# Split low halves, a norm shared with ScalarE, and a new list of steps in a Fourier transform with two MLPs on one core

## The chip, the core and the metric

The kernel runs on one core of a Trainium2 chip. The core has a matrix engine (TensorE, PE in the profile; PEld is its weight load), VectorE (DVE), ScalarE (ACT), GpSimd (POOL) and SyncE (SP), which here only issues DMAs. Each engine works through its own list of instructions in order and waits on semaphores for the others. The metric is the device time of one launch in microseconds (us), as the median of several runs.

## The reference, cut to what matters

```python
X = np.fft.fft(np.fft.fft(x, axis=1), axis=2).real            # x: 2 x 3008 x 256, float32
h = X @ w_in;  g = h * np.clip(h + 3.0, 0.0, 6.0) / 6.0;  y = g @ w_out      # w_in 256 x 2048
xn = y / np.sqrt(np.mean(y * y, -1, keepdims=True) + 1e-06) * rms_g
g2 = xn @ w_gate;  out = (g2 / (1 + np.exp(-g2)) * (xn @ w_val)) @ w_out2    # w_gate 256 x 1536
```

The weights come in as 8-byte floating point numbers and are turned into float32 on the chip ("decode").

## The kernel before, in words

Every matrix product keeps about float32 precision by splitting each operand into a high part (`S.copy` to a rounded type, on ScalarE) and a low part (`sub`, operand minus high part, on GpSimd or, for steps with a mark, on VectorE), and by three matrix multiplications: high by high, low by high, high by low (`PASSES`).

The transform along the sequence folds the 3008 points of each batch into sums and differences (`fold` for the first batch, `late_fold` and `late_split` for the second), multiplies them by tables of cosines and sines (`smm`, L435) and copies the result out of PSUM (`evac`, `evac_x`). A column that does not fit the tables (`fold_x128`, `split_x128`, `xmm`, `evac_x`) goes its own way, through `xb`. The transform along the model dimension is multiplied into `w_in` (`wmm`).

The first MLP is 96 **items** (`item1`; numbers 0 to 95 in the list of steps): six blocks of 502 columns, each with its mirrored columns, by 16 slices of 128 hidden units. An item has 6 matrix multiplications into two PSUM banks E and O (L532), a vector operation that adds the odd column (L536), a sum and a difference (L538, L539), two Relu on ScalarE (L544), two minimum-and-multiply on VectorE (L547), the high part on ScalarE (L550), the low part on GpSimd (L268, called from L553) and 12 matrix multiplications into four accumulating banks (L564).

The second MLP is 144 items (`item2`; +0 to +143 in the list): 12 blocks of 502 columns by 12 slices. Ahead of a block stands its **norm** (`rms`, rms0 to rms11): Square on ScalarE, the mean over 256 by a matrix multiplication with ones, an integer estimate of the reciprocal root, three Newton rounds of three vector operations each (L654, L656, L658), two scalings (L661), high and low part. The blocks of rms0 and rms1 serve items +0 to +23, and so these two norms lie among the last items of the first MLP.

The order of the work is not left to a scheduler: each function is a generator, and the string `STEPS` names, token by token, which one goes on to its next `yield`. An engine's instructions stand in the order in which the tokens issue them. A token with a quote mark puts the subtraction of that step on VectorE instead of GpSimd. PSUM is full: E0, O0, E1, O1 are used by items in turn, acc0 to acc3 by the sums. `sl(tag)` names a place in SBUF; a place that is taken again makes its next writer wait for the last reader. Lines L78 to L164 hold the list.

Of the kernel before, what the change touches and what calls it, by code (L numbers as in the profile page):

```python
# [13 lines left out]
ALU = mybir.AluOpType  # L14
P = 128
# [75 lines left out]
    lf2 17 16 19 18 19 18 17 lf2 19 18 19 18 20 lf2 18 19 21 20 ls00 20 21 lm01 18 20 21 19 20 22 20 ls00 21 19 22 21 20
    22 23 21 22 21 20 23 pq02 23 pq02' 23 21 22 23 22 22 24 23 25 24 24 23 22 25 24 25 24 25 23 24 25 24 26 23 27 26 25 26
# [8 lines left out]
    56 55 cw01 57 56 lw11 cw01 57 56 cw01 58 57 56 59 58 cw10 cw10 57 56 59 58 59 58 57 cw10 59 58 59 58 60 cw10 58 59
    lw20 61 60 cw10 60 cw10 61 58 60 61 59 cw11 cw10 60 cw11 62 60 61 cw11 60 59 62 61 62 63 61 cw11 62 lw21 61 60 63 pq12
    63 cw11 62 pq12 63 61 62 63 cw11 64 62 cw20 cw11 63 cw20 65 63 62 64 65 64 65 64 63 cw20 65 64 65 66 64 63 cw20 64 67
    66 66 65 67 cw20 65 64 66 67 rms0 66 cw20 67 rms0 68 66 cw20 67 65 cw21 66 68 cw21 69 67 68 67 66 69 68 cw21 69 67
    cw21 69 68 rms1 69 70 68 rms1 69 68 71 70 cw21 70 71 69 68 70 71 70 cw21 71 72 70 cw21 71 69 70 72 72 73 72 rms0 rms0
    71 70 72 71 73 73 74 72 73 72 71 74 74 73 74 72 73 74 73 75 74 74 76 75 75 73 76 75 76 75 76 74 75 76 75 77 76 78 77
    76 77 75 78 77 78 77 78 76 77 78 77 79 78 80 79 78 79 77 80 79 80 79 80 78 79 80 79 81 80 82 81 80 81 79 82 81 82 81
    82 79 rms0 82 rms0 83 81 rms0 rms0 84 81 83 rms0 80 tw1 83 81 82 84 rms0 83 82 84 83 rms0 82 84 rms0 83 rms0 84 83 85
    rms0 84 86 84 85 83 86 85 rms0 85 86 84 tw2 rms0 86 85 rms0 85 87 rms0 85 86 lw30 rms0 87 88 86 rms0 86 85 88 87 cw30
    88 87 86 cw30 88 rms1 87 rms1 89 87 cw30 88 87 89 90 88 cw30 88 87 89 lw40 cw30 90 89 90 cw30 88 89 90 89 90 89 91 90  # L110
# [57 lines left out]
def fft_mlp_mlp_kernel(ctx: ExitStack, tc: tile.TileContext, x, xq, mats, dmat, w_in, w_out, w_gate, w_val, w_out2, rms_g, out):  # L168
# [671 lines left out]
```

## Time and profile before

| | us |
|---|---|
| median of 3 runs | 1140.87 (1140.39 to 1141.67) |
| profiled execution, its own time | 1142.43 |
| its span, first to last instruction | 1140.7 |
| PE busy | 1067.5 (94%) |
| PE weight loads busy | 870.2 (76%) |
| DVE busy | 832.6 (73%) |
| ACT busy | 504.8 (44%) |
| POOL busy | 483.0 (42%) |
| mean granted TensorE clock | 0.982 |

A busy share is a mean over stages with different limits, so the rows further down cut the span into stretches. In a row of waits, "A <- B" says that engine A sat idle until the instruction of engine B ended; in a row of the timeline the bracket gives the idle time just before it. Busy times of one engine can overlap by some hundredths of a microsecond, since an instruction starts while the one before it drains.

### The profile page before, as it was taken

How to read it: one execution, taken by the hardware profiler on the slowest of the kernel's cores; microseconds unless marked ns; L12 is line 12 of the kernel's file. 1: busy time of each engine (PE TensorE's matmuls, PEld its weight loads, DVE VectorE, ACT ScalarE, POOL GpSimd, SP SyncE). 2: the span in 40 equal slices, each digit the busy share in tenths (PEclk: the TensorE clock that was granted, in tenths of full speed). 3: DMA queues.
4: the chain of work that ended last, by engine and by line, in shares of the span. 5: the costliest groups of instructions: out<-in, count | busy, mean ns of one | idle time of the engine just before them, and what ended most of it. 6: DMA issues, size and time to landing. Idle time of an engine off the chain costs nothing.

```text
span 1140.7 us, 12657 instructions
## 1 busy us (share of the span) xinstructions
PE 1067.5 (94%) x4572; PEld 870.2 (76%) x4572; DVE 832.6 (73%) x1223; ACT 504.8 (44%) x754; POOL 483.0 (42%) x292
## 2 busy tenths in 40 slices
PE   3778788999998899899999999999999999999998
PEld 3656566888886678678778888888888888888887
DVE  6899998787779997998789874383746657374532
ACT  6556435655565565455444433232323233332332
POOL 0056444656755566465234333333323333332332
PEclk9889998999999999999999999999999999999999
DMA  8640132002431100110220000000000000000000
GB/s 268 208 145 1 37 77 41 1 1 41 100 77 39 55 38 1 38 55 1 79 89 36 37 1 19 1 19 1 19 19 1 19 1 19 16 3 19 1 19 19
DMA packets 18895, 47.21 MB, mean 41 GB/s; under 512 B 3914, under 2 KB 6986, under 8 KB 17946
## 3 DMA queue, kind: packets, MB, share of 16 engines
q1 hardware_dynamic: 15808, 36.92, 9.9%
q0 software_dynamic: 3024, 9.48, 3.7%
q8 instruction: 36, 0.59, 0.2%
q14 instruction: 27, 0.22, 0.1%
HBM read 33.53 MB, written 8.27 MB: 37 GB/s over the span
## 4 chain that ended last, share of the span: by engine, by line
PE 70%; DVE 21%; issue 3%; DMA 3%; ACT 1%; POOL 1%; SPq 0%; DVEq 0%; ACTq 0%; POOLq 0%
PE acc L709 16%; PE E L687 16%; PE O L687 16%; PE acc L564 13%; DVE R L547 4%; PE E L532 3%; PE O L532 3%; DVE T L536 2%; DVE O L539 2%; DVE E L538 2%; DMA J<-in_x 1%; PE E L435 1%; PE O L435 1%; POOL LO L268 1%; DVE c_p L258 1%
## 5 line engine op out<-in xcount | busy, mean ns | idle before, releaser
L268 POOL TENSOR_TENSOR LO<-R,HI 128x1004 fp32r<-128x1004 f32 x96 | 233.8, 2448 | 193.2 <-ACT HI L550 185.4
L564 PE MATMUL acc<-HI,B 128*128 128x502 f32 x768 | 250.9, 394 | 0.1
L693 DVE TENSOR_TENSOR R<-T,E 128x502 f32<-128x502 f32 x144 | 97.2, 675 | 177.9 <-ACT T L690 173.6
L268 POOL TENSOR_TENSOR HI<-R,HI 128x502 fp32r<-128x502 f32 x87 | 119.0, 1367 | 239.0 <-ACT HI L699 238.9
L564 PEld LDWEIGHTS acc<-HI,B 128*128 128x128 f32 x768 | 147.0, 191 | 30.6 <-ACT HI L550 0.5
L564 PE MATMUL acc<-LO,B 128*128 128x502 f32 x384 | 153.5, 400 | 10.5 <-POOL LO L268 10.3
L687 PE MATMUL E<-J,B 128*128 128x502 f32 x576 | 147.3, 391 | 0.0
L687 PE MATMUL O<-J,A 128*128 128x502 f32 x576 | 146.6, 389 | 0.0
L550 ACT CAST HI<-R 128x1004 fp32r<-128x1004 f32 x96 | 99.2, 1034 | 97.6 <-DVE R L547 63.2
L268 POOL TENSOR_TENSOR LO<-R,LO 128x502 fp32r<-128x502 f32 x57 | 77.4, 1358 | 148.2 <-ACT LO L699 148.2
L690 ACT ACTIVATE T<-E 128x502 f32<-128x502 f32 x144 | 84.8, 589 | 108.4 <-PE E L687 108.2
L687 PEld LDWEIGHTS E<-J,B 128*128 128x128 f32 x576 | 108.9, 189 | 22.9
L687 PEld LDWEIGHTS O<-J,A 128*128 128x128 f32 x576 | 108.8, 189 | 22.5
L699 ACT CAST HI<-R 128x502 fp32r<-128x502 f32 x87 | 53.3, 613 | 141.3 <-DVE R L695 126.8
L544 ACT ACTIVATE R<-E,c_three 128x502 f32<-128x502 f32 x96 | 65.4, 682 | 97.7 <-DVE E L538 78.9
L532 PE MATMUL E<-J,A 128*128 128x502 f32 x288 | 86.4, 410 | 23.3 <-DVE R L547 22.6
L695 DVE TENSOR_TENSOR R<-R,O 128x502 f32<-128x502 f32 x144 | 97.1, 674 | 9.2
L564 PEld LDWEIGHTS acc<-LO,B 128*128 128x128 f32 x384 | 73.5, 191 | 34.4 <-POOL LO L268 19.7
L709 PE MATMUL acc<-HI,B 128*128 128x502 f32 x354 | 90.5, 391 | 0.0
L532 PEld LDWEIGHTS E<-J,A 128*128 128x128 f32 x288 | 55.0, 197 | 41.3 <-DVE R L547 29.7
L532 PE MATMUL O<-J,A 128*128 128x502 f32 x288 | 85.2, 406 | 0.0
L709 PEld LDWEIGHTS acc<-HI,B 128*128 128x128 f32 x354 | 66.8, 189 | 14.4 <-POOL HI L268 0.4
(233 smaller groups left out, 1643.1 us busy)
## 6 DMA issues: line engine op xcount, KB each, us to landing
out_dram<-H SPq DMA_DIRECT2D x24, 251.0 KB
A<-in_w_in SPq DMA_DIRECT2D x4, 1024.0 KB
W<-in_w_gate SPq DMA_DIRECT2D x6, 512.0 KB
W<-in_w_val SPq DMA_DIRECT2D x6, 512.0 KB
W<-in_w_out SPq DMA_DIRECT2D x6, 512.0 KB
PQ<-in_x SPq DMA_DIRECT2D x3, 1008.0 KB
B<-in_w_out SPq DMA_DIRECT2D x2, 1024.0 KB
YB<-in_w_out SPq DMA_DIRECT2D x2, 1024.0 KB
```

Source lines behind the costliest of these rows:

```text
L268: low[0].tensor_tensor(o, a, b, op=ALU.subtract)
L532: T.matmul(bk[:, :BL], a[:, lw, eo, fs], j[:, eo, lx], start=(n == 0), stop=(n == 2))
L544: S.activation(x, bk[:, :BL], AF.Relu, bias=c3)
L547: V.scalar_tensor_tensor(x, x, 6.0, bk[:, :BL], op0=ALU.min, op1=ALU.mult)
L550: S.copy(hi, r)
L564: T.matmul(acc[k][:, :BL], w[:, lw, f % 4, d * P:(d + 1) * P], (hi, lo)[lx][:, hf * BL:(hf + 1) * BL], start=(first and n == 0), stop=(las ...
L687: T.matmul(bk[:, :BL], w[:, lw, d, fs], j[:, d, lx], start=(m == 0), stop=(m == 5))
L690: S.activation(s, E[:, :BL], AF.Sigmoid)
L693: V.tensor_tensor(u, s, E[:, :BL], op=ALU.mult)
L695: V.tensor_tensor(u, u, O[:, :BL], op=ALU.mult)
L699: S.copy(hl[0], u)
L709: T.matmul(acc[d][:, :BL], w[:, lw, f % 4, d * P:(d + 1) * P], hl[lx], start=(f == 0 and m == 0), stop=(f == NF2 - 1 and m == 2))
```

## The change

Three edits in the functions, and a new list. In `item1` the low part is issued as two subtractions of 502 columns, each a step of its own, where it was one of 1004. In `rms` five operations of VectorE go to ScalarE: the high part of the sum of squares, the scaling with the added constant, and in each Newton round the product `-0.5*r*r`, which becomes `Square(sqrt(0.5)*r)` with the sign turned in the last operation of the round; three rounds turn the sign three times, and a negated copy of the gain (`gsn`) puts it right. A second constant (`ceps`) is set for the scaling. The list `STEPS` is planned anew from its first to its last line.

```diff
 STEPS = """
-    one dm x01 raw11 raw00 g xq x00 x00 raw01 lwi0 raw02 x02 raw10 fold1 fold1 mat11 fold1 fold1 mat00 fx sx0 fold1 sx0
...
+    one dm xq x01 raw00 x00 x00 raw01 g lwi0 raw02 fx x02 sx0 raw11 sx0 raw10 sx0 sx1 fold1 fold1 mat00 fold1 mat00 mat00
...
-    c3 = sl("c_three", [P, 1])
+    cc = sl("c_three", [P, 2])
+    c3, ceps = cc[:, 0:1], cc[:, 1:2]
     gsc = sl("c_g", [P, 2])
+    gsn = sl("c_gn", [P, 2])
...
         lo = sl(rr("LO", 2), [P, 2 * BL], F32R)
-        sub(lo, r, f32(hi))
-        yield
+        for x in range(2):
+            cs = slice(x * BL, (x + 1) * BL)
+            sub(lo[:, cs], r[:, cs], f32(hi[:, cs]))
+            yield
...
         hl = sl("LO2", [P, 2, BL], F32R)
-        V.tensor_copy(hl[:, 0], sm)
+        S.copy(hl[:, 0], sm)
...
-        V.tensor_scalar(v, p[:, :BL], 1.0 / D, EPS, op0=ALU.mult, op1=ALU.add)
+        S.activation(v, p[:, :BL], AF.Identity, scale=1.0 / D, bias=ceps)
...
             yield
-            V.scalar_tensor_tensor(a, r, -0.5, r, op0=ALU.mult, op1=ALU.mult)
+            S.activation(a, r, AF.Square, scale=math.sqrt(0.5))
             yield
             V.tensor_tensor(a, a, v, op=ALU.mult)
             yield
-            V.scalar_tensor_tensor(r, a, 1.5, r, op0=ALU.add, op1=ALU.mult)
+            V.scalar_tensor_tensor(r, a, 1.5, r, op0=ALU.subtract, op1=ALU.mult)
         for d in range(2):
             yield
-            V.scalar_tensor_tensor(xn[:, d], y1[blk][:, d, cs], gsc[:, d:d + 1], r, op0=ALU.mult, op1=ALU.mult)
+            V.scalar_tensor_tensor(xn[:, d], y1[blk][:, d, cs], gsn[:, d:d + 1], r, op0=ALU.mult, op1=ALU.mult)
...
         SY.dma_start(gsc, rms_g)
+        yield
+        V.tensor_scalar(gsn, gsc, -1.0, None, op0=ALU.mult)
```

Where the list moves instructions, three places matter. The first is the start of SP's list of DMAs. `in_x` is the input, `in_mats` the tables (YB and A tiles those of the even outputs, PQ1 those of the odd ones), `in_w_in` the first MLP's weights. Before:

```order
L212 DMA J1_10_83<-in_x 126x2048
L228 DMA PQ1_11_85<-in_mats 126x2268
L228 DMA YB1_12_87<-in_mats 126x2268
L732 DMA c_g_3_70<-in_rms_g 128x2
L726 DMA c_xq_6_73<-in_xq 126x48
L212 DMA J0_13_91<-in_x 126x1024 x2
L228 DMA YB2_14_94<-in_mats 126x2268
L247 DMA A1_15_96<-in_w_in 128x2x1024
```

Now:

```order
L733 DMA c_xq_7_74<-in_xq 126x48
L216 DMA J1_11_86<-in_x 126x2048
L232 DMA YB1_12_88<-in_mats 126x2268
L216 DMA J0_13_90<-in_x 126x1024 x2
L232 DMA YB2_14_93<-in_mats 126x2268
L739 DMA c_g_3_70<-in_rms_g 128x2
L251 DMA A1_15_96<-in_w_in 128x2x1024
L232 DMA A2_16_98<-in_mats 126x2268
```

The odd table (558.1 KB) no longer stands second, and the small `in_xq` stands first. The second place is TensorE's list around item 0 (the first rows `<-J0,A0`); acc0 and acc1 there are the odd column's product of the odd outputs (`xmm`), E and O with 376 columns the other products of the odd outputs. Before:

```order
L435 MATMUL O0_65_329<-YB2_68_353,YB0_55_270 128x376 x3
L435 MATMUL E1_69_356<-c_p9_74_378,YB0_55_270 128x376 x3
L435 MATMUL O1_70_357<-YB2_68_353,YB0_55_270 128x376 x3
L435 MATMUL acc0_57_276<-YB2_68_353,J1_28_136 128x376 x3
L435 MATMUL acc1_58_277<-YB2_68_353,J1_28_136 128x376 x3
L532 MATMUL E0_80_414<-J0_71_364,A0_59_284 128x502 x3
L532 MATMUL O0_81_415<-J0_71_364,A0_59_284 128x502 x3
```

Now:

```order
L439 MATMUL O0_64_319<-YB2_69_347,YB0_56_268 128x376 x3
L439 MATMUL E1_66_329<-c_p9_70_358,YB0_56_268 128x376 x3
L439 MATMUL O1_67_330<-YB2_69_347,YB0_56_268 128x376 x3
L536 MATMUL E0_76_388<-J0_65_327,A0_57_278 128x502 x3
L536 MATMUL O0_77_389<-J0_65_327,A0_57_278 128x502 x3
L536 MATMUL E1_78_399<-J0_65_327,A0_57_278 128x502 x3
L536 MATMUL O1_79_400<-J0_65_327,A0_57_278 128x502 x3
L439 MATMUL acc0_81_411<-A2_52_244,J1_23_116 128x376 x3
L439 MATMUL acc1_82_412<-A2_52_244,J1_23_116 128x376 x3
```

All 18 multiplications of that product now stand behind items 0 and 1; before, 12 of them stood earlier still and the last 6 in front of item 0. The third place is VectorE's list in the last items of the first MLP; W0 and LO2 are tiles of rms0, the rows with T, E, O and R belong to items. Before, from the first operation of item 84 to the last ahead of that of item 85:

```order
L536 SCALAR_TENSOR_TENSOR T0_704_3632<-X1_8_75,c_wx_4_71,E0_694_3585 128x502
L658 SCALAR_TENSOR_TENSOR W0_592_3039<-LO2_693_3583,W0_592_3039 128x502
L538 TENSOR_TENSOR E0_694_3585<-T0_704_3632,O0_695_3586 128x502
L539 TENSOR_TENSOR O0_695_3586<-T0_704_3632,O0_695_3586 128x502
L547 SCALAR_TENSOR_TENSOR R1_705_3635<-R1_705_3635,E1_690_3571 128x502
L547 SCALAR_TENSOR_TENSOR R1_705_3635<-R1_705_3635,O1_691_3572 128x502
L654 SCALAR_TENSOR_TENSOR LO2_693_3583<-W0_592_3039 128x502
L656 TENSOR_TENSOR LO2_693_3583<-LO2_693_3583,W0_592_3039 128x502
L658 SCALAR_TENSOR_TENSOR W0_592_3039<-LO2_693_3583,W0_592_3039 128x502
L547 SCALAR_TENSOR_TENSOR R0_707_3657<-R0_707_3657,E0_694_3585 128x502
L547 SCALAR_TENSOR_TENSOR R0_707_3657<-R0_707_3657,O0_695_3586 128x502
L654 SCALAR_TENSOR_TENSOR LO2_693_3583<-W0_592_3039 128x502
```

Now, in the same place:

```order
L540 SCALAR_TENSOR_TENSOR T0_716_3762<-X1_9_76,c_wx_5_72,E0_710_3741 128x502
L542 TENSOR_TENSOR E0_710_3741<-T0_716_3762,O0_711_3742 128x502
L543 TENSOR_TENSOR O0_711_3742<-T0_716_3762,O0_711_3742 128x502
L540 SCALAR_TENSOR_TENSOR T1_717_3779<-X1_9_76,c_wx_5_72,E1_714_3754 128x502
L542 TENSOR_TENSOR E1_714_3754<-T1_717_3779,O1_715_3755 128x502
L543 TENSOR_TENSOR O1_715_3755<-T1_717_3779,O1_715_3755 128x502
L551 SCALAR_TENSOR_TENSOR R0_718_3781<-R0_718_3781,E0_710_3741 128x502
L551 SCALAR_TENSOR_TENSOR R0_718_3781<-R0_718_3781,O0_711_3742 128x502
```

And now, twelve items earlier, from the first operation of item 72 to that of item 73:

```order
L540 SCALAR_TENSOR_TENSOR T0_630_3318<-X1_9_76,c_wx_5_72,E0_626_3291 128x502
L542 TENSOR_TENSOR E0_626_3291<-T0_630_3318,O0_627_3292 128x502
L543 TENSOR_TENSOR O0_627_3292<-T0_630_3318,O0_627_3292 128x502
L662 TENSOR_TENSOR LO2_629_3316<-LO2_629_3316,W0_578_3050 128x502
L664 SCALAR_TENSOR_TENSOR W0_578_3050<-LO2_629_3316,W0_578_3050 128x502
L540 SCALAR_TENSOR_TENSOR T1_634_3348<-X1_9_76,c_wx_5_72,E1_631_3323 128x502
```

A Newton round has two rows on VectorE where it had three, and the rounds of rms0 stand at items 72 to 74 where they stood at items 82 to 86.

## Rows read from the trace of the kernel before

**Rows 1.** windows; stretch, length, busy (count) of PE, PEld, DVE, ACT, POOL, clock, DMA, GB/s:

```profile
0.00:57.00 57.00, 30.96 (x128) 27.27 (x129) 41.74 (x77) 33.42 (x47) 4.56 (x8) 0.91 0.71 238
57.00:126.00 69.00, 58.67 (x231) 45.01 (x230) 67.01 (x87) 39.93 (x54) 41.38 (x16) 0.93 0.19 62
126.00:187.00 61.00, 44.76 (x165) 33.17 (x164) 57.45 (x80) 24.08 (x34) 27.80 (x18) 0.92 0.32 70
187.00:216.00 29.00, 29.00 (x122) 23.75 (x122) 21.61 (x34) 18.82 (x27) 16.13 (x8) 0.94 0.01 2
216.00:322.00 106.00, 106.00 (x478) 88.80 (x476) 80.62 (x129) 59.84 (x84) 66.67 (x42) 1.00 0.25 49
322.00:421.00 99.00, 89.49 (x379) 71.09 (x379) 90.05 (x132) 58.66 (x84) 61.22 (x29) 0.98 0.13 43
421.00:462.00 41.00, 41.00 (x181) 33.82 (x180) 31.24 (x51) 21.82 (x30) 24.56 (x11) 1.00 0.04 13
462.00:538.00 76.00, 70.54 (x295) 55.61 (x294) 70.66 (x103) 39.97 (x54) 39.97 (x19) 0.98 0.10 35
538.00:577.00 39.00, 38.33 (x164) 30.29 (x162) 31.81 (x50) 18.23 (x32) 12.22 (x9) 1.00 0.27 81
577.00:1140.70 563.70, 558.75 (x2443) 461.37 (x2443) 340.45 (x489) 190.08 (x313) 188.50 (x139) 1.00 0.05 16
```

**Rows 2.** DVE timeline to 60 us; start, length, instruction, idle before and releaser:

```profile
7.00 1.23 DVE L332 TENSOR_TENSOR H<-J 126x1024 f32<-126x1024 f32 x1 [5.70 <-DMA J<-in_x]
...
53.93 0.55 DVE L455 TENSOR_TENSOR PQX<-E,T 128x376 f32<-128x376 f32 x1 [4.77 <-ACT T L452]
...
56.94 0.73 DVE L536 SCALAR_TENSOR_TENSOR T<-PQX,c_wx,E 128x502 f32<-128x502 f32 x1
```

**Rows 3.** ACT timeline to 60 us:

```profile
11.82 0.82 ACT L240 CAST R<-YB 126x756 fp32r<-126x756 f16 x1 [0.95 <-DMA YB<-in_mats]
```

**Rows 4.** groups by form; line, engine, names, form, count, busy and mean ns, idle:

```profile
L268 POOL TENSOR_TENSOR LO<-R,HI 128x1004 fp32r<-128x1004 f32 x96 | 233.8, 2448 | 193.2 <-ACT HI L550 185.4 <-PE acc L564 4.9 <-issue 2.3
...
L268 POOL TENSOR_TENSOR HI<-R,HI 128x502 fp32r<-128x502 f32 x87 | 119.0, 1367 | 239.0 <-ACT HI L699 238.9
...
L547 DVE SCALAR_TENSOR_TENSOR R<-R,E 128x502 f32<-128x502 f32 x96 | 64.4, 671 | 2.9 <-ACT R L544 2.7
...
L699 ACT CAST HI<-R 128x502 fp32r<-128x502 f32 x87 | 53.3, 613 | 141.3 <-DVE R L695 126.8 <-PE acc L709 12.9 <-POOL HI L268 1.3
...
L654 DVE SCALAR_TENSOR_TENSOR LO<-R 128x502 f32<-128x502 f32 x30 | 25.3, 842 | 0.4
...
L637 DVE CAST LO<-R 128x502 fp32r<-128x502 f32 x10 | 9.5, 948 | 0.1
...
L658 DVE SCALAR_TENSOR_TENSOR W<-LO,W 128x502 f32<-128x502 f32 x6 | 7.9, 1314 | 0.0
...
L656 DVE TENSOR_TENSOR LO<-LO,W 128x502 f32<-128x502 f32 x6 | 6.7, 1114 | 0.1
...
L654 DVE SCALAR_TENSOR_TENSOR LO<-W 128x502 f32<-128x502 f32 x6 | 6.1, 1019 | 0.1
```

**Rows 5.** waits, all of the span; waiter, releaser, total us, count, longest:

```profile
PE acc L564 <- POOL LO L268: 10.3, 11, 2.0
```

**Rows 6.** DVE timeline, three places before 538 us:

```profile
65.59 2.34 DVE L263 SCALAR_TENSOR_TENSOR W<-A,W 128x1024 int32<-128x1024 int32 x1
...
144.35 2.90 DVE L343 TENSOR_TENSOR B<-W 126x256 f32<-126x256 f32 x2
147.30 3.25 DVE L332 TENSOR_TENSOR W<-PQ 126x1024 f32<-126x1024 f32 x1
...
535.10 2.81 DVE L656 TENSOR_TENSOR LO<-LO,W 128x502 f32<-128x502 f32 x1
```

**Rows 7.** POOL timeline at two of those places:

```profile
144.52 4.95 POOL L268 TENSOR_TENSOR LO<-R,HI 128x1004 fp32r<-128x1004 f32 x2 [2.84 <-ACT HI L550]
...
535.03 2.35 POOL L268 TENSOR_TENSOR LO<-R,HI 128x1004 fp32r<-128x1004 f32 x1 [4.62 <-ACT HI L550]
```

More of the change, by code (lines that the diff above doesn't have):

```diff
@@ L101 @@
[L101 to L110, printed above, removed]
@@ new lines @@
+    X00 fold0 fold1 fold0 fold1 fold0 fold1' fold1 mat01 g fold0 fold1 fold0 mat01 fold1 mat01 X01 fold0 dwi0 fold0 dwi0
+    mat02 fold0' mat02 dwi0 PQ000 mat02 fold0 X02 dwi0 fold0 PQ001 evx0 lwo0 fold2 lwi1 dwi0 PQ100 mat11 fold0' PQ101
+    fold2 mat11 mat11 dwi0' mat10 fold2 mat10 wt0 mat10 evx0 wt0 dwo0 fold2 evx0 fold2 dwo0 wt0 wt0 wt0 fold2' dwo0 PQ002
+    fold2 PQ102 ev00 dwo0 fold2 ev10 fold2' dwo0 ev00 raw12 wt0 wt0 dwo0 ev10 PQ010 wt0 pq00 PQ110 wt0 pq00' dwi1 PQ011
+    mat12 PQ111 dwi1 mat12 mat12 dwi1 PQ012 lwo3 PQ112 dwi1 ev01 ev01 ev11 lwo1 dwi1 ev11 0 sx1 dwi1 sx1 1 0 0 X10 1 0 X11
@@ new lines @@
+    1 X12 lwi3 0 1 lwo2 evx1 wt1 1 dwo1 evx1 0 2 dwo1 1 0 wt1 pq01 2 2 wt1 0 wt1 wt1 pq01' 1 0 2 wt1 wt1 wt1 2 evx1 dwi3 1
+    wt1 3 lwi2 2 dwo1 x10 2 1 3 dwi3 2 3 4 dwi3 3 2 4 dwi3 3 4 5 3 dwo1 3 4 5 dwo1 4 3 5 6 4 dwo1' 4 5 3 6 dwi2 5 4 6 7 5
+    dwi2 6 5 4 7 6 5 7 8 6 dwi2 7 6 5 8 7 6 8 9 7 dwi2 8 7 6 9 dwi2 8 7 9 10 8 dwi2 9 7 10 10 8 dwo2 9 8 7 dwo2 11 10 8
+    dwo2 9 11 dwo2 9 11 dwo2 9 10 dwo2' 9 11 lf0 10 10 11 wt2 lf0 10 11 wt2 lf0 11 wt2 10 wt2 wt2 wt2 wt2 dwi3 wt2 11
+    dwi3' wt2 12 x11 13 12 dwo3 12 11 dwo3 12 13 12 13 14 12 dwo3 12 13 14 13 12 14 15 13 dwo3 13 14 12 15 dwo3 14 13 15
@@ new lines @@
+    62 cw20 65 64 64 63 62 65 63 64 65 64 65 63 64 65 rms0 64 66 63 rms0 64 67 66 65 66 cw20 64 67 65 66 cw20 67 65 cw21
+    66 65 67 cw21 66 cw21 67 66 68 cw21 67 66 pq12 69 67 68 cw21 66 69 67 68 pq12 69 68 67 69 68 cw21 69 68 cw21 70 68 69
+    71 70 68 70 69 68 71 70 69 71 rms0 70 71 69 rms0 70 71 70 rms0 71 70 72 rms0 71 70 rms0 71 72 rms0 72 73 rms0 72 71
+    rms0 73 rms0 72 rms0 72 74 73 rms1 72 74 73 rms1 72 74 73 72 74 rms0 73 74 rms0 73 75 rms0 74 73 76 rms0 74 73 75 76
+    74 75 76 75 74 rms0 76 75 76 77 75 rms0 75 76 78 77 lw30 77 75 78 76 75 77 78 76 cw30 77 78 cw30 79 cw30 77 78 76 rms0
@@ new lines @@
+    77 79 cw30 77 79 lw40 80 78 rms0 79 78 77 80 rms1 79 78 80 81 79 rms1 80 79 78 81 81 79 80 81 79 80 81 80 82 81 80 79
+    83 81 82 82 81 80 83 82 tw1 83 82 83 81 82 83 82 84 82 83 83 85 84 84 83 82 85 84 85 84 85 83 84 85 84 rms1 85 86 84
+    rms1 87 85 86 86 85 84 cw30 87 86 cw30 87 86 87 85 86 87 86 rms1 88 87 86 89 88 88 87 86 89 87 88 89 88 89 87 88 89
+    rms1 88 rms1 90 89 88 91 90 90 89 88 91 89 90 91 90 91 89 90 91 90 rms1 92 91 90 93 92 92 91 90 93 91 92 93 92 93 91
+    92 93 92 94 93 92 95 94 tw2 94 93 92 95 93 94 95 94 95 93 94 95 94 +0 95 94 95 94 +0 95 rms1 +0 +0 rms1 +1 rms1 +0 +0
@@ new lines @@
+    +41 rms4 +42 +39 rms4 rms5 +39 rms5 +35 +42 +41 +41 +36 +40 +35 +35 +40 rms5 +43 +35 +41 +35 rms5 +41 +42 +42 +37 +43
+    +43 +44 +42 +43 +42 +38 +44 +44 +45 +43 +44 +43 +39 +45 +45 +46 +44 +45 +44 +40 +46 +46 +47 +45 +46 +45 +41 +47 +47
+    +48 +46 +47 +46 +42 +48 +48 +49 +47 +48 +47 +43 +49 +49 +50 +48 +49 +48 +44 +50 +50 +51 +49 +50 +49 +45 +51 +51 rms5
+    +50 +51 +46 rms5 +50 rms5 +52 +51 +51 +47 +52 +52 +48 +47 +52 +47 +47 +52 +53 rms5 +47 +52 +49 +53 +53 +54 rms5 +53
+    rms5 +53 rms5 +53 +50 rms5 +54 +54 +55 rms5 +54 rms5 +54 +54 +51 +55 +55 +56 +55 +55 +55 +52 +56 +56 +57 rms5 +56 +56
@@ new lines @@
+    +102 +101 +102 rms10 +103 +102 rms9 rms10 +102 rms9 +102 +100 +103 rms10 +103 +104 +103 +103 +103 +101 +104 +104 +105
+    rms10 +104 +104 +104 +102 +105 +105 +106 +105 +105 +105 +103 +106 +106 +107 +106 +106 +106 +104 +107 +107 +108 +107
+    +107 +107 +105 +108 +108 +109 +108 +108 +108 +106 +109 +109 +110 +109 +109 +109 +107 +110 +110 +111 +107 +110 +107
+    +107 +110 +107 +110 +108 +111 +111 rms10 +111 +109 rms10 +111 rms10 +112 +111 rms10 rms10 rms10 +113 rms10 +112 rms10
+    +112 rms10 +112 rms10 +110 +113 rms10 +112 +113 +114 +112 rms10 +113 rms10 +111 +113 rms10 +114 +113 +114 rms11 +115
```

113 lines of the change are left out of this document (51 added, 62 removed), and 18 rows, old and new, of the table STEPS.

## The prediction, made before the changed kernel ran

> **What bounds the kernel now.** I read four views in this order: the page's busy table, the windows, the groups by form, the timelines at the marks. The busy table says PE 94%, VectorE 73%: the kernel as a whole is TensorE's. The windows [rows 1] say where this fails. Their marks are the first vector operations of items 0, 12, 22, 28, 52, 72 and 82 and of item +0 of the second MLP (57, 126, 187, 216, 322, 421, 462 and 538 us), so one row is the time from one mark to the next. In 187–216, 216–322 and 421–462 PE is busy for the whole stretch: TensorE sets the time, and VectorE has room (21.61 of 29, 80.62 of 106, 31.24 of 41). In 57–126, 126–187 and 462–538 VectorE is busy 97%, 94% and 93% while PE loses 10.3, 16.2 and 5.5 us: VectorE sets the time. In 322–421 it is mixed (PE 89.49, DVE 90.05 of 99). Before 57 us neither is: 26 us of PE and 15 of VectorE are idle. After 538 PE loses 0.7 and 5.0 us in 603. So of the 73.2 us that PE is idle, 67 lie ahead of the second MLP, and only there can VectorE's work be worth much. Norms later on run beside a full PE.
>
> **Two ways of weighing.** VectorE's work between two marks I take as the count of each kind of instruction in the program's order, before and now, times the mean of that kind in the trace; such sums stand a few per cent above the busy time, since neighbours overlap. PE's work goes likewise at 0.2285 us per multiplication of 502 columns, its spacing in the full stretches.
>
> **The change, stretch by stretch.**
>
> *Start to item 0.* VectorE's work falls from 46.1 to 44.0: the second pair of additions for the odd column goes behind item 0 (-1.1) and a subtraction goes to POOL (-1.2); PE gives up 18 multiplications of 376 columns. VectorE's last long wait there is the 4.77 us at 53.93 for ScalarE's copy of PE's result [rows 2]. Now four decode operations (about 3.5 us) stand ahead of that wait, so some 2 us of it are filled. SP issues the even table one load of 558 KB earlier; ScalarE's first cast, which waits for that table at 11.82 [rows 3], may come up to 1.8 us earlier, my estimate from the KB ahead of it at the stretch's 238 GB/s [rows 1] (558/238 = 2.3 us, less the small loads now ahead). The column's fold gets into the 5.70 us before 7.00 [rows 2]. 2.1 + 2 + 1.4 = 5.5: **-5.5** at 56.94; bounds -2 (only VectorE's work) and -8.
>
> *Items 0 to 12.* VectorE's work grows from 70.2 to 75.2: the deferred additions (+1.1), a subtraction of J1 taken from a later place (+1.5), two of 128x1024 on VectorE instead of POOL (+2.4). At 97% nothing hides it: 5.0 times 0.93 (67.01 busy stood for 70.2 summed, and part replaces waits) gives **+4.6**; bounds 0, if the 2 us of idle take half and the items run less delayed, and +5.
>
> *Items 12 to 28.* Held-back folds: VectorE's work falls from 64.4 to 57.2 between items 12 and 22, and rises from 23.4 to 30.4 between 22 and 28, where it had 7.4 us free [rows 1]. TensorE's 29.0 there stays the bound if the work lands in the holes. That takes 7.2 off the VectorE-bound part; I take **-6**, since 30.4 (some 28 busy) in 29 leaves no slack; bounds -7 and -2.
>
> *Items 28 to 52.* PE is the bound; its work grows by the copies of the folds' products moved in here, 105.0 to 108.1: **+3.1**. VectorE 88.3 to 88.8 is hidden.
>
> *Items 52 to 72.* VectorE 93.8 to 94.4, PE unchanged at 85.2: **+0.6**.
>
> *Items 72 to 82.* Eleven operations of rms0 stand here instead of two (+9.5), and four decodes (+3.1): VectorE 34.1 to 47.9 against PE's 41.1. At the ratio 31.24/34.1 [rows 1] that is 43.9 busy, so VectorE becomes the bound; with its usual 4% of idle 45.5: **+4.5**; bounds +1 and +7.
>
> *Items 82 to +0.* The norm's operations here fall from 25 to 4 (-20.5), the decodes go (-3.1), items -1.3: VectorE 76.3 to 51.4. PE's work falls from 63.8 to 57.9 (some of it comes earlier, above, and some later, below). So PE takes over; with 2.4 of loss, half of what it loses here now, the stretch goes from 75.5 to 60.3: **-15.2**; bounds -10 and -16. The means I took off are those of this place, 1019, 1114 and 1314 ns [rows 4]; the same `-0.5*r*r` costs 842 later on.
>
> *Behind +0.* 12 multiplications of the last items now follow +0's first: 12 x 0.2285 = **+2.7**. Of the 5.6 us that PE still loses there I give back **-1**: each norm has five instructions of VectorE fewer (the count between +0 and +28 goes from 41 to 23). The rest of the 47.5 us that VectorE is relieved of in all lies beside a full PE: nothing.
>
> *The halves.* 96 subtractions of 2448 ns become 192 of about 1367, the same form in the second MLP [rows 4]: POOL gets 96 x (2734 - 2448) = 27 us more, of 657 us in which it is idle. The first half is there 1.08 us earlier. PE waits for this operation 11 times, 10.3 us in all [rows 5], all in stretches that VectorE sets, so an earlier half moves a wait rather than ends it: 0, bounds -3 and +2 of the plain wait; what the halves do to VectorE is weighed among the rivals.
>
> *ScalarE.* It gets five operations a norm at some 0.6 us, near its copy of the same size, 613 [rows 4], about 36 us in all with 636 idle. It gives 948 ns of VectorE's copy for 613 of ScalarE's [rows 4]. The Trainium skill, "ScalarE: Activation LUTs", section "Rules for kernel authors", says to put multiplications and additions on VectorE, not ScalarE, as much as 3 times faster in bf16; by that rule a moved product would take no less on ScalarE than its 842 on VectorE, 0.23 us more than I took, which over the ten moved operations of the two norms ahead of +0 makes the sum -10. The trace has float32 from SBUF: 842 and 948 against 613, so it does not agree, and the sum goes by the trace.
>
> The sum: -5.5 + 4.6 - 6 + 3.1 + 0.6 + 4.5 - 15.2 + 2.7 - 1 = **-12.2**. The profiled execution took 1142.43 (span 1140.7, the rest around it), so 1130.2 for its like; the median of the runs is 1.56 lower, 1128.7. I forecast **1129 us**, own range 1124 to 1134.
>
> **The rivals.**
>
> *The halves take less of VectorE's time (about 1120).* A row with two inputs from SBUF that meets a running POOL operation ends when that one ends: the L656 at 535.10 takes 2.81 us beside POOL's 535.03 to 537.38, the L332 at 147.30 takes 3.25 where at 7.00 the same form took 1.23 [rows 2, 6, 7]. Over their undisturbed length, 33 such operations up to 538 (the first 65.59, the last 535.10 [rows 6]) cost 42.6 us. A piece half as long would hold such a row up half as long: up to 21 us, of which 29.5 of the 42.6 lie in stretches that VectorE sets, so some 8 to 10 beyond the forecast. Against it: the next piece follows at once.
>
> *Slower, by the same port (about 1148).* POOL's two pieces stand back to back. If a row that waits for the first is caught by the second also, it loses what it lost before plus the extra 2 x 1.367 - 2.448 = 0.29 us; if two rows in a row are caught, one by each piece, where before one waited and the next ran free, 1.08 us more each. 144.35 (two operations, 2.90) and 147.30 (3.25) beside POOL's pair of 4.95 [rows 6, 7] show how back-to-back POOL operations catch one after another. By the shares of the 42.6 us some 23 of the 33 held rows lie in VectorE's stretches; with 18 of them caught twice it is 19 us, 1148; from 11 on the gain is gone. Against it: rows with an operand in PSUM are not held (96 L547 in items beside POOL, mean 671 [rows 4]), and most of VectorE's rows are such. The Trainium skill, "GPSIMD Engine Reference", section "8. Key points", says that POOL shares its SBUF interfaces with VectorE and contends with its instructions of two SBUF inputs; by this rule a POOL 27 us busier is a cost. The trace agrees that there is contention: 3.25 against 1.23 for one form.
>
> *No gain to see (about 1138).* The norms now go to ScalarE and back five times each. In 462–538 VectorE stood at 0.1 us of idle ahead of its own L654 to L658 rows [rows 4]; with ScalarE between, each hand-over may wait behind a 1.03 us high part or two Relus, up to 1.6 us x 5 x 2 norms = 16 us; half of it in stretches that count brings back 8 to 9 of the 12. For it: L654's row was queued at once behind its predecessor. Against it: item rows stand between, and ScalarE is idle about half of 462–538.
>
> **How the numbers follow.** Forecast 0.57, the port's gain 0.15, no gain to see 0.17, slower 0.11. A measurement of this kernel tells 0.2%, 2.3 us. Faster by more: 0.57 + 0.15 and a third of the third case, 0.78; slower 0.11 and its lowest edge, 0.12; the rest 0.10. The range holds 8 in 10 from 1119 to 1140: the forecast, nearly all of the gain's case, and no gain; the slow case is left out.
>
> **What would show it.** Right: item 0's vector operation near 51.5 us, item 28's near 209, item 72's near 418, item 82's near 463.5, the first vector operation of +0 near 524; PE without idle in the last stretch; 0.6 us for ScalarE's `Square` of 502. Wrong: item 72 to 82 past 48 us (then the norm has only been moved), two long VectorE rows in a row beside POOL's pieces, waits of VectorE for ScalarE at L664, PE idle for norms of +24 and later, or item 0 no earlier than 55.

## The result, and the profile after

The changed kernel takes 1112.47 us (1110.82 to 1114.03, four runs) against 1140.9: a ratio of 0.975, 95% interval 0.9733 to 0.9767, so 28.4 us faster. The forecast was 1129, and its range ended at 1119: the direction was right, but the forecast gain of 12 us was less than half of the measured one. The profiled execution took 1110.82, with a span of 1109.1. The two profiled executions lie 31.6 us apart, 3.2 more than the medians, since the one before was slower than its median and this one faster.

The windows of the changed kernel at the same marks (columns as in [rows 1]: stretch, length, then PE, PEld, DVE, ACT, POOL busy with counts, granted clock, DMA share, GB/s):

```profile
0.00:49.80 49.80, 27.59 (x107) 23.18 (x108) 40.64 (x76) 30.72 (x43) 5.04 (x8) 0.97 0.70 233
49.80:119.20 69.40, 61.80 (x256) 48.56 (x255) 68.36 (x90) 42.22 (x58) 42.88 (x26) 0.95 0.30 92
119.20:168.60 49.40, 42.03 (x168) 32.48 (x167) 46.60 (x74) 24.24 (x33) 25.57 (x20) 0.93 0.23 61
168.60:196.70 28.10, 27.22 (x117) 21.23 (x116) 26.56 (x41) 17.71 (x26) 18.95 (x14) 1.00 0.00 1
196.70:307.10 110.40, 109.42 (x495) 91.62 (x494) 81.86 (x133) 62.05 (x89) 76.84 (x72) 1.00 0.30 62
307.10:398.60 91.50, 89.35 (x387) 72.09 (x386) 85.74 (x134) 58.63 (x84) 66.22 (x50) 1.00 0.13 47
398.60:442.90 44.30, 40.31 (x168) 30.68 (x167) 42.56 (x66) 26.77 (x37) 25.24 (x18) 1.00 0.04 12
442.90:503.50 60.60, 60.60 (x267) 49.77 (x266) 47.40 (x74) 37.64 (x53) 41.54 (x35) 1.00 0.11 35
503.50:542.00 38.50, 38.15 (x168) 31.21 (x167) 29.13 (x46) 19.00 (x34) 13.17 (x10) 1.00 0.25 83
542.00:1109.10 567.10, 561.28 (x2457) 463.10 (x2455) 304.26 (x443) 218.28 (x364) 185.28 (x138) 1.00 0.05 16
```

What is read from it is the length of each stretch against that of [rows 1], beside the terms of the forecast. The last column is an experiment's, l_norm below: the new list and the new norm, but the low part in one piece, which the forecast, with its zero for the halves, in fact described. All differences are between profiled spans, in us, with the marks taken to the hundredth ([rows 1] has them rounded to whole us).

| stretch | forecast | changed kernel | new list and norm, one piece |
|---|---|---|---|
| start to item 0 | -5.5 | -7.2 | -6.0 |
| items 0 to 12 | +4.6 | +0.6 | +2.3 |
| items 12 to 28 | -6 | -12.7 | -12.0 |
| items 28 to 52 | +3.1 | +4.2 | +4.6 |
| items 52 to 72 | +0.6 | -7.6 | -2.2 |
| items 72 to 82 | +4.5 | +3.2 | +8.0 |
| items 82 to +0 | -15.2 | -15.0 | -13.8 |
| behind +0 | +1.7 | +2.7 | +2.8 |
| sum, from the spans | -12.2 | -31.6 | -16.3 |

Item 0's vector operation stands at 49.8 (51.5 was forecast), item 82's at 442.9 (463.5), +0's at 503.5 (524). In 442.9–503.5 PE is busy for the whole 60.60: the bound did change over to TensorE there, as forecast, though the forecast had made up its 60.3 of 57.9 of work and 2.4 of idle time, so that only their sum was met.

The second thing to read is how long VectorE's rows last beside POOL. Four pieces of POOL, one after another, each in a row of its own:

```profile
311.60 1.27 POOL L272 TENSOR_TENSOR LO<-R,HI 128x502 fp32r<-128x502 f32 x1 [1.43 <-ACT HI L554]
312.82 1.46 POOL L272 TENSOR_TENSOR LO<-R,HI 128x502 fp32r<-128x502 f32 x1
314.25 1.46 POOL L272 TENSOR_TENSOR LO<-R,HI 128x502 fp32r<-128x502 f32 x1
315.67 1.72 POOL L272 TENSOR_TENSOR LO<-R,HI 128x502 fp32r<-128x502 f32 x1
```

and VectorE's rows beside them:

```profile
312.11 1.04 DVE L262 TENSOR_SCALAR c_p<-c_p 128x512 f32<-128x512 f32 x1 [0.54 <-ACT c_p L260]
313.19 1.38 DVE L263 TENSOR_SCALAR c_p<-c_p 128x512 int32<-128x512 int32 x1
314.49 1.75 DVE L640 TENSOR_TENSOR R<-R 128x502 f32<-128x502 f32 x1
```

The first ends 0.28 us behind the end of the first piece (313.15 against 312.87), the second 0.29 behind the second's, the third 0.53 behind the third's. A row waits for the piece that runs when it starts, then does its own work, although the next piece of POOL is already due; that piece is longer instead (1.46 and 1.72 against 1.27). So here each row pays for one piece. The first two of these rows are a `TENSOR_SCALAR`, with a single tensor from SBUF as input: it isn't only rows with two such inputs that are held.

I call a row's **excess** its length over the shortest one of the same source line and form, counted from 0.15 us on. Up to item +0 the excess was 42.2 us in 31 rows before (the prediction counted 42.6 in 33); it is 25.3 us in 34 rows now. The largest single one fell from 2.16 to 1.10 us. In both kernels exactly one subtraction of POOL ends while such a row runs, for each of the 31 and of the 34 rows, and none of the rows has an operand in PSUM.

### The profile page after: what moved, and what is told of

Same layout as the page of the kernel before. It is cut to its first block, busy times and chain, and to the rows that moved or that the text cites. A ratio compares the mean times of both kernels' runs of the same rounds, so it can differ in the third digit from the quotient of the medians.

```text
span 1109.1 us, 12686 instructions
## 1 busy us (share of the span) xinstructions
PE 1057.7 (95%) x4572; PEld 863.9 (78%) x4572; DVE 773.1 (70%) x1169; ACT 537.3 (48%) x814; POOL 500.7 (45%) x384
## 2 busy tenths in 40 slices
DMA packets 18895, 47.21 MB, mean 43 GB/s; under 512 B 3914, under 2 KB 6986, under 8 KB 17946
## 4 chain that ended last, share of the span: by engine, by line
PE 68%; DVE 19%; POOL 4%; issue 4%; ACT 3%; DMA 2%; SPq 0%; DVEq 0%; ACTq 0%; POOLq 0%
PE acc L715 16%; PE O L693 16%; PE E L693 16%; PE acc L570 13%; PE E L536 3%; POOL LO L272 3%; DVE R L551 3%; PE O L536 3%; DVE T L540 2%; DVE O L543 2%; DVE E L542 2%; DVE c_p L265 1%; DMA J<-in_x 1%; DVE c_p L267 1%; DVE c_p L262 1%
## 5 line engine op out<-in xcount | busy, mean ns | idle before, releaser
L272 POOL TENSOR_TENSOR LO<-R,HI 128x502 fp32r<-128x502 f32 x192 | 261.6, 1390 | 156.3 <-ACT HI L554 156.2
L554 ACT CAST HI<-R 128x1004 fp32r<-128x1004 f32 x96 | 98.9, 1034 | 75.4 <-PE acc L570 37.7
L570 PEld LDWEIGHTS acc<-LO,B 128*128 128x128 f32 x384 | 72.8, 190 | 25.0 <-POOL LO L272 10.3
```

Source lines behind the costliest of these rows:

```text
L272: low[0].tensor_tensor(o, a, b, op=ALU.subtract)
L554: S.copy(hi, r)
L570: T.matmul(acc[k][:, :BL], w[:, lw, f % 4, d * P:(d + 1) * P], (hi, lo)[lx][:, hf * BL:(hf + 1) * BL], start=(first and n == 0), stop=(las ...
```

## The experiments

Times are medians; a ratio is to the kernel before, run on the same chip, whose median was 1141.5 to 1142.0 in every group. Four theories stand against each other. A: a shorter piece of POOL holds VectorE's rows up for less. B: the list alone made the gain that was not forecast. C: pieces that stand back to back catch a row twice. D: TensorE gains because the first half is there sooner.

**Halves alone (h_only).** The kernel before and its own list.

```diff
-        sub(lo, r, f32(hi))
+        for x in range(2):
+            cs = slice(x * BL, (x + 1) * BL)
+            sub(lo[:, cs], r[:, cs], f32(hi[:, cs]))
         yield
```

> The kernel before, its own list; only the item's low part is issued as two subtractions of 502 columns in the same step. Theory A (shorter holds): VectorE's rows that meet a POOL subtraction are held by a piece half as long, so the 42 us of excess up to 538 us fall to some 24, and of the part that lies where VectorE sets the time about 8 to 12 us come off: 1129 to 1133. Theory B (the list alone made the unforecast gain, by placing work in other holes): 1139 to 1142. Theory C (back-to-back pieces catch a row twice): over 1145.

1127.61 us, ratio 0.9877 (0.9864 to 0.9891): -14.3, more than theory A had (8 to 12), and far from B and C. Here the instructions stand as before, so single rows can be compared with [rows 6, 7]. VectorE's timeline:

```profile
142.04 1.82 DVE L343 TENSOR_TENSOR B<-W 126x256 f32<-126x256 f32 x2
143.90 2.17 DVE L332 TENSOR_TENSOR W<-PQ 126x1024 f32<-126x1024 f32 x1
```

and POOL's:

```profile
142.21 6.24 POOL L268 TENSOR_TENSOR LO<-R,HI 128x502 fp32r<-128x502 f32 x4 [2.85 <-ACT HI L550]
```

The same two lines (the first stands for two instructions) took 2.90 and 3.25: each is 1.08 us shorter, which is the difference of a piece of 2.448 and one of 1.367. POOL's four pieces take 6.24 us where the two took 4.95. The excess up to +0 falls from 42.2 to 27.2, by 15.0 us; the time falls by 14.3. Stretch by stretch the two go together: items 12 to 22 lose 4.1 us of excess and become 4.4 shorter, items 52 to 72 lose 4.0 and become 4.8 shorter, items 82 to +0 lose 2.9 and become 3.4 shorter; only in items 0 to 12 does less come off (1.8) than the excess loses (4.4). The other stretches stay within 0.6 us.

**New list and norm, low part whole (l_norm); new list and halves, norm on VectorE (l_halves); new list alone (l_only).** Each takes parts of the change back out of the changed kernel:

```diff
-        for x in range(2):
-            cs = slice(x * BL, (x + 1) * BL)
-            sub(lo[:, cs], r[:, cs], f32(hi[:, cs]))
-            yield
+        sub(lo, r, f32(hi))
+        yield
+        yield
```

```diff
-        S.copy(hl[:, 0], sm)
+        V.tensor_copy(hl[:, 0], sm)
...
-            S.activation(a, r, AF.Square, scale=math.sqrt(0.5))
+            V.scalar_tensor_tensor(a, r, -0.5, r, op0=ALU.mult, op1=ALU.mult)
```

> The changed kernel with its list and its norm, but the low part again as one subtraction of 1004 columns, issued where the first half stood. Theory A: the gain that the forecast missed was the halves', so this comes out near the forecast, 1125 to 1131. Theory B: the halves matter little, 1112 to 1117.

> The changed kernel with its list and its halves, but the five operations of each norm back on VectorE. The forecast took 13.6 us of VectorE's time off each norm that lies where VectorE bounds. If the norm's transfer matters only for the two norms ahead of item +0: 1117 to 1123, the loss between items 72 and 95. If ScalarE's hand-overs cost as much as they give: 1111 to 1114.

> The changed kernel's list alone: the low part in one subtraction, the norm on VectorE. Theory A: both functions' gains are missing, the list by itself gives little: 1132 to 1141. Theory B: the list gives most of the 28 us: 1115 to 1122.

l_norm 1125.99 (0.9855, 0.9838 to 0.9872); l_halves 1115.36 (0.9769, 0.9756 to 0.9782); l_only 1129.45 (0.9897, 0.9882 to 0.9912). l_norm falls where theory A put it. l_halves lies between its two windows, 2.9 above the changed kernel, and the loss is where its first one looked for it, in items 72 to 82 (48.1 us against 44.3). l_only is in neither theory's window: the list by itself gives 12.5, less than B and more than A said. Two rows of l_norm, items 52 to 72 and 72 to 82, show what one piece costs on the new list:

```profile
310.95:407.80 96.85, 90.58 (x388) 71.81 (x387) 90.68 (x133) 58.93 (x84) 62.07 (x29) 1.00 0.13 44
407.80:457.00 49.20, 41.31 (x168) 32.06 (x167) 47.21 (x67) 26.95 (x37) 21.23 (x9) 0.97 0.04 11
```

VectorE does the same work as in the changed kernel but is busy 90.68 and 47.21 instead of 85.74 and 42.56, and the stretches are 5.4 and 4.9 us longer.

**Norm alone (n_only), halves and norm (h_norm), on the old list.** The diff is that of the norm in the change; the negated gain is made in the first step of rms0.

> The kernel before, its own list; only the five operations of each norm go to ScalarE. If VectorE's time in items 82 to 95 is what counts, ten operations of 0.7 to 1.3 us go there and 4 to 9 us come off: 1132 to 1137. If the hand-overs to ScalarE cost as much, since this list was not planned for them: 1139 to 1146.

> The kernel before, its own list; halves and the norm on ScalarE together. Halves alone gave -14.3 (1127.6). If the two add up and the norm is worth 4 to 9: 1119 to 1124. If they overlap (both shorten VectorE's work at the same norm's rows) or the hand-overs eat it: 1125 to 1130.

n_only 1139.45 (0.9978, 0.9969 to 0.9987): -2.5, just inside the second window, and less than the 4 to 9 of the first. In items 82 to +0 VectorE waits 2.7 us there for ScalarE's results of the norm. h_norm 1123.81 (0.9841, 0.9828 to 0.9855), which is 3.8 below h_only, at the edge of its first window. The norm's transfer is worth 2.5 and 3.8 us on the old list, 3.5 and 2.9 on the new one (the 2.9 hardly clear of the intervals). The stretch in which most of the two norms' rows stand became 3.1 us (n_only) and 3.2 us (h_norm against h_only) shorter in items 82 to +0, and 3.3 (l_norm against l_only) and 3.8 us (the changed kernel against l_halves) shorter in items 72 to 82.

On the old list items 22 to 28 also became about 1.5 us shorter with the same 121 multiplications, though no norm stands there: the kernel before enters that stretch with a granted clock of 0.53 in its first 3 us, near the lower level (1.2 GHz), n_only and h_norm with 1.00, the upper one (2.4 GHz). Ahead of it PE was busy 45.0 of 61.3 us in the kernel before and 44.7 of 61.2 in n_only, so the cause of that difference stays open. It is part of the 2.5 and the 3.8, and hardly the transfer's.

With the eight corners of halves, norm and list all measured, the parts add up: 14.3 + 2.5 + 12.5 = 29.3 against 28.4 and, measured again (after_again), 28.9.

**Second half first (second_first on the changed kernel, h_second_first on h_only).** TensorE wants the first half first, so it now waits for both; the pieces stay as long.

```diff
-        for x in range(2):
+        for x in (1, 0):
```

> The changed kernel, but POOL makes the second half first, so that TensorE, which wants the first half first, waits until both are there; the pieces are as long as before. Theory A (the pieces' length counts, for what they hold up on VectorE): 1111 to 1114, the excess of VectorE's rows up to item +0 unchanged near 24 us. Theory D (the first half being there 1.1 us sooner counts, for TensorE): TensorE's waits for POOL go back from 4.3 towards 13 us, and the time to 1117 to 1122.

> The kernel before and its own list with halves (1127.6 so far), the second half first. Theory A: 1127 to 1129. Theory D: about half of the 14.3 comes back as with the new list, 1132 to 1136, and TensorE's waits for POOL go from 3.4 towards 10 us.

second_first 1119.14 (0.9798, 0.9783 to 0.9813): 6.7 us come back, in theory D's window, with TensorE's waits for POOL at 12.0 us and the excess at 27.5. h_second_first 1130.13 (0.9898, 0.9885 to 0.9912) lies between its two windows, nearer to A's: only 2.5 of 14.3 come back, although TensorE's wait there (waits view: waiter, releaser, total us, count, longest) is longer than in the kernel before, nearly twice that of [rows 5]:

```profile
PE acc L566 <- POOL LO L268: 19.3, 18, 2.2
```

So on the old list the wait hardly matters and the holds do; on the new one both do.

**Low parts multiplied last (lolast_whole on l_norm, lolast on the changed kernel, lolast_before on the kernel before).** TensorE's twelve products of an item in another order, which gives POOL more time and leaves VectorE's rows alone:

```diff
-        for k in range(4):
-            hf, d = divmod(k, 2)
-            for n, (lw, lx) in enumerate(PASSES):
+        for k, n in [(k, n) for k in range(4) for n in (0, 2)] + [(k, 1) for k in range(4)]:
+            hf, d = divmod(k, 2)
+            lw, lx = PASSES[n]
```

> The changed list and norm with the low part in one subtraction (1126.0 so far), but TensorE multiplies the four low parts of an item last, after the eight products of the high part, so that POOL has 8 x 0.2285 = 1.8 us longer. VectorE's held rows stay as they are. Theory D (what counts is when TensorE gets the low part): 1119 to 1122, TensorE's waits for POOL down from 13.2 to under 4 us. Theory A (the length of the hold): 1124 to 1127 although those waits go.

> The changed kernel with its halves, but TensorE multiplies the low parts of an item last. If what is left of TensorE's waits for POOL (4.3 us, and 10.3 of its weight loads) still costs: 1108 to 1111. If it lies where VectorE sets the time: 1111 to 1114.

> The kernel before with nothing but the low parts multiplied last. TensorE's 10.3 us of waits for POOL go, VectorE's 42 us of excess stay. By what the changed list showed (6.2 with the low part whole): 1135 to 1138. By the old list's own order of halves (2.5 between first and second first): 1138 to 1141.

lolast_whole 1119.81 (0.9808, 0.9794 to 0.9821): 6.2 below l_norm, as theory D said, with the excess at 37.7 against 38.6. TensorE's waits for POOL in l_norm,

```profile
PE acc L569 <- POOL LO L272: 13.2, 12, 2.3
```

fall to 2.3 us, and of its weight loads' waits (21.1) this is left:

```profile
PEld acc L569 <- POOL LO L272: 4.7, 6, 1.1
```

lolast 1110.38 (0.9727, 0.9714 to 0.9741) is in the first of its windows, but the 2.2 us that it lies below the changed kernel are less than the two intervals tell apart. Between lolast_whole and lolast, where TensorE hardly waits for POOL (2.3 and 2.6 us), the halves still give 9.4 us, and the excess falls from 37.7 to 27.1. lolast_before 1140.96 (0.9995, 0.9986 to 1.0004): no gain to be told, though TensorE's waits for POOL fall from 10.3 to 0.7 us. So on the old list they were worth nothing, as the forecast had it. One caution: there POOL waits longer for TensorE to give the low part's buffer back,

```profile
POOL LO L268 <- PE acc L564: 20.0, 6, 4.1
```

against 4.9 before, and some of a gain may have gone into that.

**Which of the two second_first lost (lolast_second_first), and the changed kernel again (after_again).**

> The changed kernel with the low parts multiplied last and POOL making the second half first. If second_first lost its 6.7 us because TensorE waited for a later half, the order of the halves matters little once TensorE wants them last: 1110 to 1113. If it lost them by other rows being held on VectorE, they stay lost: 1115 to 1119.

> The changed kernel once more, as the measure for the others of this group: 1111 to 1114.

after_again 1112.59 (0.9744, 0.973 to 0.9758). lolast_second_first 1110.66 (0.9721, 0.9707 to 0.9735), as lolast: once TensorE wants the low parts last, the order of the halves is free. So second_first's 6.7 go with TensorE's wait (12.0 us there, 4.3 in the changed kernel, 2.7 here).

**Quarters (quarters on the changed kernel, lolast_quarters on lolast).**

```diff
-            cs = slice(x * BL, (x + 1) * BL)
-            sub(lo[:, cs], r[:, cs], f32(hi[:, cs]))
+            for h in range(2):
+                cs = slice(x * BL + h * BL // 2, x * BL + (h + 1) * BL // 2)
+                sub(lo[:, cs], r[:, cs], f32(hi[:, cs]))
```

> The changed kernel, but the low part in four subtractions of 251 columns, two in each step. A piece's fixed part is 2 x 1.367 - 2.448 = 0.29 us, so a quarter takes about 0.83 us, and POOL works 55 us more than with halves. Theory A: a held row loses at most some 0.6 us instead of 1.1, the excess up to +0 falls from 24 to about 14 us, unless it is caught again by the next piece: 1106 to 1113. Theory C (back-to-back pieces catch rows repeatedly): no gain or a loss, 1113 to 1120.

> The changed kernel with the low parts multiplied last and made in quarters. In quarters the excess fell by some 8 us but TensorE and ScalarE waited longer for the later last piece. If TensorE's part of that was what ate the gain: 1105 to 1109. If it is ScalarE, which waits for POOL to give R back: 1109 to 1113.

quarters 1111.09 (0.9733, 0.9719 to 0.9746), not to be told from the changed kernel; lolast_quarters 1109.26 (0.9713, 0.97 to 0.9727), the fastest measured, 3.3 below after_again on the same chip. The excess falls to 16.9 and 17.6, as a shorter piece should make it, but ScalarE's Relu now waits for POOL to give R back. In quarters:

```profile
ACT R L548 <- POOL LO L272: 67.3, 45, 3.0
```

against 33.3 us in 27 waits in the changed kernel. The last expectation asked which of TensorE and ScalarE ate the gain; at 1109.3 it lies at the border of its two answers, and that stays open.

**Only the folds held back (hn_folds).** h_norm with its own list, in which only the late steps of the second batch stand later, as in the new list:

```diff
 STEPS: highest item number seen before the token
-lf0 14 14   lf1 15 15 15 15 16   x12 15  lm00 15  lf2 17 17 19 19 20  ls00 21 22  lm01 21
+lf0 17 17   lf1 17 18 19 20 20   x12 20  lm00 20  lf2 21 22 24 25 27  ls00 34 35  lm01 34
```

> The kernel before with halves and norm (1123.8 so far) and its own list, in which alone the second batch's late steps are moved: two steps of the first fold from item 14 to 17, the second fold from 15 to 17-20, its load and table with it, the third from 17-20 to 21-27, and two splits from 21-22 to 34. If holding the folds back makes the 12 us that items 12 to 28 became shorter, 6 to 10 us come off: 1114 to 1118. If it only moves VectorE's work: 1122 to 1126.

1125.42 (0.9856, 0.9843 to 0.987), 1.6 above h_norm: no gain. Items 12 to 22 and 22 to 28 in hn_folds:

```profile
123.90:181.50 57.60, 42.81 (x170) 32.72 (x169) 51.45 (x72) 23.94 (x33) 27.94 (x22) 0.93 0.19 46
181.50:212.40 30.90, 29.77 (x125) 23.57 (x124) 28.10 (x43) 17.51 (x26) 16.43 (x12) 0.97 0.00 1
```

and the same two in h_norm:

```profile
123.80:182.00 58.20, 45.51 (x170) 33.70 (x169) 53.66 (x81) 24.18 (x34) 31.51 (x26) 0.91 0.30 63
182.00:209.30 27.30, 27.30 (x121) 22.61 (x120) 21.65 (x33) 18.65 (x27) 17.77 (x16) 1.00 0.04 6
```

VectorE's work went over as meant (81 and 33 rows became 72 and 43), but the first stretch became only 0.6 us shorter and the second 3.6 longer; VectorE's excess in the second rose from 0.3 to 4.5. In the first stands the longest held row of all runs, and it met two pieces (its row in VectorE's timeline, then theirs in POOL's):

```profile
172.36 3.69 DVE L334 TENSOR_TENSOR W<-PQ 126x1024 f32<-126x1024 f32 x1
172.51 2.45 POOL L270 TENSOR_TENSOR LO<-R,HI 128x502 fp32r<-128x502 f32 x2
```

It ends 1.09 us behind the second piece, where at 7.00 the same form took 1.23 [rows 2]. So theory C's case does occur, but hardly ever: among all held rows of the kernels with halves up to +0 this is one of two (the other is in l_halves, at 392.11).

## Why the prediction was wrong

**The step that failed** is "*The halves.*", which the forecast took at 0 with bounds -3 and +2. Measured they are worth 14.3 us on the old list and 13.4 on the new one. The forecast looked for a gain of TensorE's, in its 10.3 us of waits, and left what the halves do to VectorE to the rivals: it priced the step by the wrong engine. That reading was right for the old list (lolast_before: no change). The gain was VectorE's: a row whose operands all lie in SBUF and that met the low part waited for a piece of 2.448 us, and now waits for one of 1.367. h_only shows it in single rows (1.08 us each), in the sum (excess -15.0, time -14.3) and stretch by stretch, and h_second_first shows it with TensorE's wait made longer instead of shorter. On the new list it is two effects: 6.2 us is TensorE's wait (l_norm to lolast_whole; second_first puts 6.7 of it back), and 9.4 us are left for the holds when that wait is gone (lolast_whole to lolast). The two overlap, since together they give 13.4; with TensorE's waits left at 12.0 us (l_norm to second_first) the holds give 6.9.

**The rival that was right** had the chance 0.15: "The halves take less of VectorE's time". Its count of 33 rows and 42.6 us was near (31 and 42.2), and its mechanism was right. Half of that, 21 us, was too much, since POOL's other subtractions stay whole and hold rows as before, and more rows were caught: h_only has 36 and 15.0 us less. Its price of 8 to 10 on the new list, for which it shows no working beyond the 29.5 of 42.6 in VectorE's stretches, fits the 9.4 that the holds alone give; that the halves would also shorten TensorE's waits on the new list, which makes it 13.4, it had not. Its counter-argument, "the next piece follows at once", kept its chance small and does not hold: nearly every row pays for one piece and goes ahead of the next.

**The rival on the slower side** fell by the same rows: pieces in a chain do catch row after row (312.11, 313.19, 314.49), each for one piece, but the number of rows caught rose only from 31 to 34, and none of the 34 met two pieces. The Trainium skill, "GPSIMD Engine Reference", section "8. Key points", names the contention of POOL with VectorE's rows of two SBUF inputs. The trace agrees, and holds rows with one SBUF input too (312.11, 313.19), which the prediction's account left out; but POOL's low parts became 27.8 us busier (233.8 to 261.6) and VectorE lost 17 us less: what counted was the length of a single piece. The same section of the Trainium skill names rows in a 2-port perf mode beside those of two SBUF inputs; no view here shows a row's mode. The length counts by what "SBUF — State Buffer", another page of the Trainium skill, has in its section "SBUF: two separate sides": whichever starts first has the pair for its whole instruction, and the other waits. The trace agrees, with 1.08 us less for a piece 1.08 us shorter; the prediction weighed only the first page.

**The list.** "*Items 12 to 28*" was taken at -6 with a bound of -7; the list and the norm without the halves made it -12.0. I had costed the moved folds at their mean lengths, and these means hold the excess of the old places: 11.7 us in 7 rows in items 12 to 22 before, 3.6 in 2 rows in l_norm, at the same length of piece (items 22 to 28: 0.3 before, 3.3 in l_norm). That holding the folds back is what saves the time fell with hn_folds: there they went to the later stretch and met POOL's pieces again. The traces show fewer rows beside a POOL piece; that the list's order of these steps against the items' low parts is the cause I did not test by itself.

**The other terms.** Start -7.2 for -5.5, inside its bounds: VectorE's wait of 4.77 us ahead of item 0 [rows 2] is gone. Items 28 to 52 +4.2 for +3.1. Items 82 to +0: -15.0 for -15.2, with the bound gone over to PE. Items 72 to 82 came out at +8.0 without the halves, past the bound of +7, since rms0's rows there met whole pieces (7.4 us of excess in l_norm, none before); with the halves +3.2. Items 0 to 12 did not hold: +2.3 without the halves for +4.6. Nor did items 52 to 72, -2.2 without the halves for +0.6. So the list and the norm in one piece came out at 1126, near the forecast of 1129, in part by luck: its stretches were off by up to 6.0 us to the faster side and 3.5 to the slower.

**The norm.** The forecast took ten operations off VectorE ahead of +0 and put them where PE sets the time or VectorE has room; most of that was the list moving them, which l_only has as well. The transfer to ScalarE itself is worth 2.5 to 3.8 us. ScalarE's Square took 0.62 us, the 0.6 that was assumed. But the 842 and 948 ns that the prediction set against it are means with holds in them. In the kernel before, most of these products take 0.67 us and the shortest of these copies 0.41 on VectorE, beside 0.62 and 0.61 on ScalarE now: left alone by POOL, the product gains little by the transfer and the copy takes longer. So the prediction's "it does not agree" rests on rows that POOL had held up. The rows of the hand-over:

```profile
L662 DVE TENSOR_TENSOR LO<-LO,R 128x502 f32<-128x502 f32 x30 | 25.5, 851 | 13.5 <-ACT LO L660 12.8
...
L660 ACT ACTIVATE LO<-R 128x502 f32<-128x502 f32 x30 | 18.7, 624 | 23.2 <-DVE R L664 19.7 <-DVE R L655 3.5
...
L662 DVE TENSOR_TENSOR LO<-LO,W 128x502 f32<-128x502 f32 x6 | 6.0, 1004 | 1.5 <-ACT LO L660 1.5
```

The hand-over's price, the rival "no gain to see", is in the last column of the rows of L662: VectorE waits 12.8 us for these Squares in ten norms, behind +0 and beside a full PE, and 1.5 us in the two norms that the rival meant (W0 and W1), only 0.5 of it ahead of +0, where the rival had up to 16. It did not take the gain.

## What to carry to other kernels

Ask of a long instruction on POOL not only who waits for its result but whom it holds up while it runs: compare the longest and the shortest row of one form on VectorE, and set them beside POOL's. If the long ones end just behind POOL's, cutting POOL's instruction into pieces may pay although it makes POOL busier. It has an end: quarters shortened the holds again and gained nothing that could be told. And a mean length of a form is a price of the places where it stood; a step that is moved is priced at its undisturbed length plus what it will meet.

## What the runs showed of the hardware that was not expected

A VectorE row held by POOL ran right after the piece in front of it, before the rest of a chain of pieces (ends 0.28, 0.29 and 0.53 us behind a piece's end), and the following POOL piece was longer for it, 1.46 to 1.72 us against 1.27. In two cases a row had to wait for two pieces (hn_folds at 172.36, l_halves at 392.11). Held were rows whose operands all lie in SBUF, those with one input too (`TENSOR_SCALAR`, 1.04 and 1.38 us at 312.11 and 313.19 where the shortest of their form takes 0.42); rows with an operand in PSUM were not: of the item's rows on VectorE, all of which read PSUM, 248 began in the kernel before while a subtraction of POOL ran, and none took 0.1 us more than the shortest of its form. The prediction had said that the row "ends when that one ends"; it ends later, by a little less than its own undisturbed length (0.28, 0.29 and 0.53 us for rows of 0.42, 0.42 and 0.67). A low part cut in halves cost POOL 0.33 us more (2 x 1390 against 2448 ns).
